# A pooled attention with a gated feed-forward on one core: full-row selections and a re-ordered prologue

## The chip, the core and the metric

The kernel runs on one core of a Trainium2 chip. The metric is device time in microseconds (us) from start to end of one execution. A core has five engines that run their own instruction queues in order and wait for each other through semaphores: TensorE (PE; its weight loads are shown apart as PEld), VectorE (DVE), ScalarE (ACT), GpSimd (POOL) and SyncE (SP). DMAs are issued from the queues of SP, ACT and POOL.

## The reference

Eight batches, eight heads, 576 tokens, head size 64. Keys and values are averaged over groups of eight tokens, so 72 pooled rows remain for each head. The queries attend to them, and the result goes through a feed-forward layer with the activation h / (1 + exp(-h)).

```python
def _attn_ref(q, k, v):
    B, H, S, D = q.shape
    pool = 8
    Sp = S // pool
    scale = 1.0 / np.sqrt(D)
    k_p = k.reshape(B, H, Sp, pool, D).mean(axis=3)
    v_p = v.reshape(B, H, Sp, pool, D).mean(axis=3)
    scores = scale * np.matmul(q, k_p.transpose(0, 1, 3, 2))
    scores = scores - np.max(scores, axis=-1, keepdims=True)
    attn = np.exp(scores)
    attn = attn / (np.sum(attn, axis=-1, keepdims=True) + 1e-09)
    return np.matmul(attn, v_p).astype(np.float32)

def _moe_ref(x, w_in, w_out):
    h = x @ w_in
    g = h * (1.0 / (1.0 + np.exp(-h)))
    return (g @ w_out).astype(np.float32)

def reference(**kwargs):
    ...
    B, H, S, D = attn_out.shape
    x = np.ascontiguousarray(attn_out.transpose(0, 2, 1, 3)).reshape(B * S, H * D)
    return _moe_ref(x=x, **moe_kwargs)
```

The model width is 512, the hidden width 2048, and there are 4608 tokens.

## The kernel before

The tokens are cut into nine tiles of 512 (`NTT`). A tile t is multiplied with `w_in` (function `up`, 16 blocks g of 128 hidden units, Silu on ScalarE into `h_T`), then with `w_out` (`down` for t = 0, `down_quarters` after it, which forms sums of quarters so that seven products do for eight). While tile t goes through these, the attention of batch t + 1 is computed as filler work: a list of (step, function) pairs, where a step is one matmul of the main work. The order of instructions on each engine is therefore the order in which the Python code issues them. The attention of batch 0 stands alone ahead of everything; this is the prologue, written out by hand between the loads and the loop over t (the lines after `act_copy`).

Pooling is done in two ways. For batches 0 to 2 the 576 rows (head, pooled position) of k or v are laid on the 128 partitions in five slots: four full ones and a last one with 64 rows (`SLOTS` = 4, `REST` = 64, `SA` = 3 slots in the first tile, two in the second). `slot_sums` (L274, L278) adds the eight tokens on DVE by halving: for the first three slots 768, 384 and 192 elements a partition, for the last two 512, 256 and 128. Then TensorE picks the rows of each head: `select_k` (L296) multiplies columns of an identity matrix with the sums, and `select_v` (L314) does the same with a shifted identity. A head's 72 rows can lie in two slots (`segments`), so four heads take twelve (k, two halves of a head) or six (v) matmuls. Where a piece lies in the last slot, the matmul has 64 rows, else 128. `a` = 0 or 1 is the half of the heads; only a = 1 reaches the last slot. For batches 3 to 7 pooling is done on 72 partitions and `k_transpose` (L222) transposes the keys on TensorE with 72 rows, into a bf16 PSUM tile.

The attention of a part of the queries is: `q_transpose` (L153, DVE), `scores` (L351, then four exponentials on ACT, L359, one for each s), `denominators` (L369, then a logarithm and an exponential on ACT, L378 and L379, or a reciprocal on DVE, L375), `numerators` (L395, then a multiplication on DVE, L404, into `xT`). In the prologue a part is (head half g, query half f). `copy_k` (L303) and `copy_v` (L321) bring the selected rows from PSUM to SBUF, on ACT or DVE.

PSUM has eight banks: three for the tag `mm`, five for `at`. `warm_up(n)` (L704) issues n matmuls of 128 x 512 on a zero tile whose result nobody reads; they keep TensorE active in the prologue.

In the loop, t = 0 cuts its first `GA` = 11 blocks g in two: the tokens of the first query half (288) for all eleven, then the other 224 for all eleven, then the remaining five blocks with 512. It begins when only the first query half is done. The denominators and numerators of the second half are fillers in it. Before the first Silu, ACT loads another table (L414).

The DMAs of q, of the weights and of part of k and v are issued from GpSimd's queue in program order. An issue on it waits until the DMA eight places before it has landed.

Of the kernel before, what the change touches and what calls it, by code (L numbers as in the profile page):

```python
# [27 lines left out]
FP32 = mybir.dt.float32  # L28
# [8 lines left out]
def kernel(  # L37
# [9 lines left out]
    nc = tc.nc  # L47
# [43 lines left out]
    def ps_tile(shape, dtype, tag, name):  # L91
        return psum.tile(shape, dtype, tag=tag, bufs=banks[tag], name=name)

    shifts = singles.tile([128, SP + 128 + SP], BF16, name="shifts")
    ident = shifts[:, SP : SP + 128]
    ones = singles.tile([SP, 32], BF16, name="ones")
    warm = singles.tile([128, 512], BF16, name="warm")
    w_in_sb = singles.tile([128, KF, d_ff], BF16, name="w_in_sb")  # L100
    w_out_sb = singles.tile([128, KG, d_model], BF16, name="w_out_sb")
    w_sum = singles.tile([128, 5, KQ, CQ], BF16, name="w_sum")
# [14 lines left out]


    kz = [singles.tile([128, 2, 2, SP], BF16, name=f"kz{n}") for n in range(2)]
    gate = singles.tile([128, 1], FP32, name="gate")  # L120

    batches = {}

    def load_q_half(b, f):
        for a in range(2):
            es = slice(f * QF * D, (f + 1) * QF * D)
            nc.gpsimd.dma_start(out=batches[b]["q_bf"][:, a, es], in_=q_r[b][:, a, es])
# [71 lines left out]
    def pool_k(b, stage):  # L199
        st = batches[b]  # L200
        raw = st["k_raw"]
        if stage == 0:
            add_halves(raw)
            return
        st["kp"] = mid.tile([SP, 2, 2, 4, DH], BF16, tag="kp", bufs=1, name="kp")
        for i in range(2):
            add_rest(
                st["kp"][:, i].rearrange("k c s d -> k s c d"), raw[:, 4 * i : 4 * (i + 1)]
            )

    def pool_v(b):
# [4 lines left out]

    def k_transpose(b, parts=(0, 1)):
        st = batches[b]
        kT_ps = ps_tile([128, 2, 2, SP], BF16, "at", "kT_ps")
        for a in parts:  # L220
            for c in range(2):
                nc.tensor.transpose(  # L222
                    kT_ps[:, a, c, :],
                    st["kp"][:, a, c].rearrange("k s d -> k (s d)"),
                    ident[:SP, :SP],
                )
        a0, a1 = parts[0], parts[-1] + 1
        nc.scalar.copy(kz[b % 2][:, a0:a1], kT_ps[:, a0:a1])
# [37 lines left out]
                in_=src[128 * i0 : 128 * i1].rearrange("(i r) e -> r i e", r=128), **how  # L266
            )

    def slot_sums(name, j, halves=False):
        raw = row_tiles[name][j]  # L270
        dst = rows5[name][:, SA:] if j else rows5[name][:, :SA]
        w = RE // 4 if halves else RE // 2
        while w > D:
            nc.vector.tensor_add(  # L274
                out=raw[..., :w], in0=raw[..., :w], in1=raw[..., w : 2 * w]
            )
            w //= 2
        nc.vector.tensor_add(out=dst, in0=raw[..., :D], in1=raw[..., D : 2 * D])  # L278


    def segments(h):
        r = SP * h
        while r < SP * (h + 1):
            i = r // 128
            e = min(SP * (h + 1), 128 * (i + 1))
            yield i, (128 if i < SLOTS else REST), r - 128 * i, r - SP * h, e - r
            r = e

    def select_k(b, a):
        st = batches[b]  # L290
        if a == 0:
            st["kz_ps"] = ps_tile([128, 2, 2, SP], FP32, "at", "kz_ps")
        for c in range(2):
            for s in range(4):
                for i, n, r, sp, m in segments(4 * a + s):
                    nc.tensor.matmul(  # L296
                        st["kz_ps"][32 * s : 32 * (s + 1), a, c, sp : sp + m],
                        lhsT=k5[:n, i, c * DH : (c + 1) * DH],
                        rhs=ident[:n, r : r + m], start=True, stop=True,
                    )  # L300

    def copy_k(b, a, copy=nc.vector.tensor_copy):
# [2 lines left out]
    def select_v(b, a, tag="at"):  # L305
        st = batches[b]
        if a == 0:
            st["v_ps"] = ps_tile([128, H, D], FP32, tag, "v_ps")
            st["vp"] = mid.tile([SP, H, D], BF16, tag="vp", name="vp")
        for h in range(4 * a, 4 * (a + 1)):  # L310
            segs = list(segments(h))
            for j, (i, n, r, sp, m) in enumerate(segs):
                x = SP + r - sp
                nc.tensor.matmul(  # L314
                    st["v_ps"][:SP, h, :], lhsT=shifts[:n, x : x + SP], rhs=v5[:n, i],
                    start=(j == 0), stop=(j == len(segs) - 1),
                )

# [21 lines left out]
            yield g, i0, i1, slice(o, o + n)  # L340
            o += n

    def scores(b, segs):
        st = batches[b]
        w = width(segs)
        sc = [ps_tile([128, 512], FP32, "at", "sc_ps")[:SP, :w] for s in range(4)]
        for g, i0, i1, cs in seg_cols(segs):
            for c in range(2):
                for s in range(4):
                    rows = slice(32 * s, 32 * (s + 1))  # L350
                    nc.tensor.matmul(  # L351
                        sc[s][:, cs],
                        lhsT=kz[b % 2][rows, g, c, :],
                        rhs=st["qT"][rows, g, i0:i1, c, :],
                        start=(c == 0), stop=(c == 1),
                    )
        es = mid.tile([SP, 4, VW], BF16, tag="es", bufs=4, name="es")[:, :, :w]
        for s in range(4):
            nc.scalar.activation(es[:, s, :], sc[s], func=AF.Exp, scale=score_scale)  # L359
        st["es", segs] = es  # L360

# [340 lines left out]
    def warm_up(n):  # L702
        for _ in range(n):
            nc.tensor.matmul(warm_ps, lhsT=warm[:, :128], rhs=warm, start=True, stop=True)  # L704

    load_slots(nc.sync, 0, "k", 0, 2)
    load_slots(nc.scalar, 0, "k", 2, 3)
    load_slots(nc.scalar, 0, "k", 3, 4)
# [1 line left out]
    load_q(0, halves=True)  # L710
    load_q_half(0, 0)
    load_slots(nc.gpsimd, 0, "v", 0, 3)
    load_q_half(0, 1)
    load_slots(nc.gpsimd, 0, "v", 3, 4)
    load_slots(nc.gpsimd, 0, "v", 4, 5)
    attn_tables()
    nc.vector.memset(warm, 0.0)
    nc.vector.memset(ones, float(POOL))
    nc.gpsimd.memset(shifts, 0.0)
    make_identity(nc, ident, nomemset=True)  # L720

# [14 lines left out]
        load_w_in(512 * c, 512 * (c + 1))  # L736

    act_copy = nc.scalar.copy
    warm_up(19)
    slot_sums("k", 0)  # L740
    select_k(0, 0)
    copy_k(0, 0, act_copy)
    warm_up(4)
    q_transpose(0, 0, 0)
    scores(0, part(0, 0))
    slot_sums("k", 1)
    warm_up(3)
    select_k(0, 1)
    copy_k(0, 1, act_copy)
    q_transpose(0, 1, 0)  # L750
    warm_up(2)
    scores(0, part(1, 0))
    denominators(0, part(0, 0))
    slot_sums("v", 0)
    warm_up(2)
    select_v(0, 0, "mm")
    copy_v(0, 0, act_copy)
    denominators(0, part(1, 0))
    q_transpose(0, 0, 1)
    scores(0, part(0, 1))  # L760
    slot_sums("v", 1)
    warm_up(1)
    numerators(0, part(0, 0), ("mm", "at"))
    warm_up(2)
    select_v(0, 1, "mm")
    copy_v(0, 1)
    q_transpose(0, 1, 1)
    warm_up(2)
    numerators(0, part(1, 0), ("mm", "at"))
    scores(0, part(1, 1))  # L770
# [18 lines left out]
    for t in range(NT):  # L789
        a = t + 1  # L790
        f_up, f_down = [], []
        if t == 0:
            GA = 11
            items = [(g, 0, HS) for g in range(GA)]
            items += [(g, HS, NTT - HS) for g in range(GA)]
            items += [(g, 0, NTT) for g in range(GA, KG)]
            f_up += [(1, lambda: denominators(0, part(0, 1), on_dve=True))]
            f_up += [(5, lambda: denominators(0, part(1, 1), on_dve=True))]
            f_up += [(13, lambda: numerators(0, part(0, 1)))]
            f_up += [(17, lambda: numerators(0, part(1, 1)))]  # L800
        else:
            G = lambda *gs: [(g, 0, NTT) for g in gs]
            if t == 1:
                items = (
                    G(12, 13, 14, 15) + [(0, "251")] + G(8) + [(0, "43")] + G(9)
                    + [(0, "7h6")] + G(10) + [(0, "s")] + G(11, 0, 1, 2, 3)
                )
            else:
                items = (
                    G(12, 13) + [(0, "251")] + G(14) + [(0, "43")] + G(15) + [(0, "76")]  # L810
                    + [(1, "2")] + [(0, "hs")] + [(1, "51")] + G(0) + [(1, "43")] + G(1)
                    + [(1, "7h6")] + G(2) + [(1, "s")] + G(3)
                )
            for n in U_X:
                f_up.append((0, lambda n=n: unit_x_sum(t, n)))
            for n in (2, 5):
                f_up.append((36 if t > 1 else 45, lambda n=n: hidden_sum(n, 4, 8)))
            f_up.append((56, lambda: hidden_sum(6, 4, 8)))
            for n, k0 in ((2, 0), (5, 0), (1, 4), (1, 0)):
                f_up.append((64, lambda n=n, k0=k0: hidden_sum(n, k0, k0 + 4)))  # L820
            f_down.append((33, lambda: hidden_sum(7, 0, 8)))
            f_down.append((71, lambda: hidden_sum(6, 0, 4)))
# [99 lines left out]
```

The softmax here doesn't subtract the row's maximum and nothing guards it: scores larger than these inputs give would overflow.

## Time and profile before

| | us |
|---|---|
| median of 3 runs | 286.77 |
| lowest and highest | 286.44 and 287.31 |
| the profiled execution's own time | 286.69 |
| its span, first to last instruction | 284.8 |

The busy times by stage, from a view that cuts the span where the stages change; the columns are the stretch, its length, and each engine's busy time with the number of instructions:

| stretch, us | what | PE busy | DVE | ACT | POOL |
|---|---|---|---|---|---|
| 0 to 22.2 | prologue, first hp blocks | 19.95 | 16.06 | 11.39 | 15.08 |
| 22.2 to 34.7 | t = 0, up | 12.45 | 9.57 | 9.06 | 4.74 |
| 34.7 to 47.5 | t = 0, down | 12.59 | 5.65 | 9.24 | 4.48 |
| 47.5 to 53.8 | end of t = 0 | 6.22 | 6.21 | 1.76 | 2.16 |
| 53.8 to 68 | t = 1, up | 13.97 | 12.61 | 10.40 | 3.56 |
| 68 to 84 | t = 1, down | 16.00 | 13.19 | 10.97 | 3.57 |
| 84 to 284 | t = 2 to 8 | 196.86 | 161.82 | 131.01 | 18.57 |

A busy time of PE counts its dummies, and matmuls overlap, so it is not useful work. Mean granted TensorE clock of the span: 1.000. GpSimd's rows in the prologue are almost all DMA issues. How to read the profile: the chain of waits is followed back from the last instruction to what released it each time, so what stands in it sets the end; the timeline gives start, length and the idle time before a row and who ended it; the DMA issues give the time from issue to landing.

### The profile page before, as it was taken

Reading aid. Unit: us, or ns where it says so; the run is one execution under the profiler, and the core shown is the slowest. Engines: PE = TensorE matmul, PEld = TensorE weight load, DVE = VectorE, ACT = ScalarE, POOL = GpSimd, SP = SyncE. Lnnn points to the kernel's source line nnn. Section 1 sums busy time; section 2 is a strip of 40 time slices with the busy share of each in tenths; the row PEclk is TensorE's granted clock in tenths of the full one; section 3 lists DMA queues with packets and bytes.
Section 4 is the critical chain, followed back from the end, with each engine's and each line's share of the span. In section 5 each row is a group of like instructions: output and inputs, shape, how many; then the busy total and the mean of one; then the engine's idle time right before and its main releaser. Section 6 shows DMA issues by size and latency. Waiting matters only on the chain.

```text
span 284.8 us, 6920 instructions
## 1 busy us (share of the span) xinstructions
PE 278.0 (98%) x2773; PEld 196.0 (69%) x2793; DVE 225.1 (79%) x403; ACT 183.8 (65%) x359; POOL 52.2 (18%) x68
## 2 busy tenths in 40 slices
PE   8989999999999999999999999999999999999995
PEld 3348544465777677767888886677677867787684
DVE  4887854979969796979698969986998686836773
ACT  1577676458656886688568857794779558325700
POOL 8664317402030011101200101054100000000000
PEclk9999999999999999999999999999999999999999
DMA  7999999793849565964895396839970032005004
GB/s 211 277 266 227 219 306 183 214 199 70 153 69 210 124 96 95 145 148 126 140 177 156 72 147 113 176 59 170 150 142 0 2 85 65 2 9 139 1 3 147
DMA packets 35296, 37.70 MB, mean 132 GB/s; under 512 B 9952, under 2 KB 27616, under 8 KB 35264
## 3 DMA queue, kind: packets, MB, share of 16 engines
q0 software_dynamic: 21760, 20.86, 43.0%
q1 hardware_dynamic: 12928, 15.48, 22.2%
q10 hardware_dynamic: 576, 0.92, 0.9%
q8 instruction: 22, 0.36, 0.6%
q14 instruction: 10, 0.08, 0.1%
HBM read 36.70 MB, written 9.44 MB: 162 GB/s over the span
## 4 chain that ended last, share of the span: by engine, by line
PE 94%; DVE 3%; ACT 1%; issue 1%; DVEq 0%
PE hp_ps L547 25%; PE o_psP L655 15%; PE o_psQ L655 15%; PE u_psQ L488 7%; PE u_psP L488 7%; PE o_psR L655 5%; PE sc_ps L351 4%; PE warm_ps L704 4%; PE o_ps L582 3%; PE nu_ps L395 3%; PE u_psR L488 2%; PE den_ps L369 2%; DVE w_sum L633 1%; PE kz_ps L296 1%; DVE xT L404 1%
## 5 line engine op out<-in xcount | busy, mean ns | idle before, releaser
L547 PE MATMUL hp_ps<-xT,w_in_sb 128*128 128x512 bf16 (+3 forms) x397 | 80.8, 338 | 1.4 <-ACT h_T L553 0.4
L655 PEld LDWEIGHTS <-h_sum 128*128 128x128 bf16 x640 | 60.6, 98 | 11.9 <-issue 1.3
L553 ACT ACTIVATE h_T<-hp_ps 128x512 bf16<-128x512 f32 (+2 forms) x95 | 51.4, 546 | 26.3 <-PE hp_ps L547 24.9
L547 PEld LDWEIGHTS <-w_in_sb 128*128 128x128 bf16 x412 | 39.3, 98 | 25.0 <-issue 1.4
L615 DVE TENSOR_TENSOR h_sum<-h_T 128x1024 bf16<-128x1024 bf16 (+1 forms) x72 | 50.8, 743 | 7.0 <-ACT h_T L553 7.0
L359 ACT ACTIVATE es<-sc_ps 72x384 bf16<-72x384 f32 (+1 forms) x100 | 39.0, 470 | 10.0 <-PE sc_ps L351 9.9
L488 PEld LDWEIGHTS <-w_sum 128*128 128x128 bf16 x300 | 29.4, 98 | 7.7
L655 PEld LDWEIGHTS <-h_T 128*128 128x128 bf16 x256 | 24.1, 98 | 4.4 <-issue 0.9
L404 DVE TENSOR_TENSOR xT<-nu_ps,rec 128x384 bf16<-128x384 f32 (+1 forms) x50 | 24.0, 532 | 0.3
L378 ACT ACTIVATE lnd<-den_ps 128x384 f32<-128x384 f32 (+1 forms) x23 | 11.1, 484 | 20.2 <-PE den_ps L369 20.2
L153 DVE STREAM_TRANSPOSE qT<-q_bf 128x576 bf16<-128x576 bf16 x32 | 23.0, 753 | 0.0
L182 POOL DMA_DIRECT2D raw<-in_k_dram x5 | 7.0, 1398 | 79.2 <-DVE h_sum L615 28.8
L496 ACT ACTIVATE h_T<-c_sb 128x512 bf16<-128x512 f32 x30 | 18.1, 625 | 5.0 <-DVE c_sb L520 5.0
L274 DVE TENSOR_TENSOR raw<-raw 128x384 f32<-128x384 f32 (+3 forms) x20 | 12.4, 618 | 7.5 <-DMA raw<-in_v_dram 4.3
L655 PE MATMUL o_psP<-w_out_sb,h_sum 128*128 128x256 bf16 x128 | 17.6, 273 | 0.0
L655 PE MATMUL o_psQ<-w_sum,h_sum 128*128 128x256 bf16 x128 | 16.7, 273 | 0.0
L655 PE MATMUL o_psQ<-w_out_sb,h_sum 128*128 128x256 bf16 x128 | 16.6, 273 | 0.0
L655 PE MATMUL o_psQ<-w_sum,h_T 128*128 128x256 bf16 x128 | 16.5, 273 | 0.0
L655 PE MATMUL o_psP<-w_sum,h_T 128*128 128x256 bf16 x128 | 16.5, 273 | 0.0
L520 DVE TENSOR_TENSOR c_sb<-u_psP,t_sb 128x512 f32<-128x512 f32 x15 | 10.2, 678 | 7.1 <-PE u_psP L488 3.6
L655 PE MATMUL o_psR<-w_sum,h_sum 128*128 128x256 bf16 x128 | 15.7, 273 | 0.0
L655 PE MATMUL o_psP<-w_sum,h_sum 128*128 128x256 bf16 x128 | 15.4, 272 | 0.0
(77 smaller groups left out, 417.1 us busy)
## 6 DMA issues: line engine op xcount, KB each, us to landing
out_dram<-o_sb SPq DMA_DIRECT2D x128, 64.0 KB, 3.0
q_bf<-in_q_dram POOLq DMA_DIRECT2D x6, 576.0 KB, 11.1
raw<-in_k_dram SPq DMA_DIRECT2D x6, 512.0 KB, 5.0
raw<-in_k_dram POOLq DMA_DIRECT2D x5, 576.0 KB, 9.1
raw<-in_v_dram POOLq DMA_DIRECT2D x5, 576.0 KB, 8.6
raw<-in_v_dram SPq DMA_DIRECT2D x5, 512.0 KB, 7.6
w_in_sb<-in_moe_w_in_dram POOLq DMA_DIRECT2D x8, 256.0 KB, 8.4
w_out_sb<-in_moe_w_out_dram POOLq DMA_DIRECT2D x4, 512.0 KB, 13.5
```

The lines of the kernel that those rows point to most:

```text
L153: nc.vector.transpose(out=st["qT"][:, a, f * QF : (f + 1) * QF].rearrange("r i c p -> r (i c p)"), in_=st["q_bf"][:, a, f * n : (f + 1) * n],)
L274: nc.vector.tensor_add(out=raw[..., :w], in0=raw[..., :w], in1=raw[..., w : 2 * w])
L351: nc.tensor.matmul(sc[s][:, cs], lhsT=kz[b % 2][rows, g, c, :], rhs=st["qT"][rows, g, i0:i1, c, :], start=(c == 0), stop=(c == 1),)
L359: nc.scalar.activation(es[:, s, :], sc[s], func=AF.Exp, scale=score_scale)
L404: nc.vector.tensor_mul(out=xT[:, 2 * g0 + c : 2 * (g0 + ng - 1) + c + 1 : 2, cols], in0=nu[c][:, :w].rearrange("r (g n) -> r g n", g=ng), ...
L488: nc.tensor.matmul(ps[bank][:, u, :], lhsT=w[:, kk, 128 * u : 128 * (u + 1)], rhs=x[:, kk, :], start=first and u == 0 and kk == 0, stop=kk ...
L496: nc.scalar.activation(h_T[:, g : g + 2, j * NQ : (j + 1) * NQ], src, func=AF.Silu)
L547: nc.tensor.matmul(hp_ps[:, r0:r1], lhsT=w_in_sb[:, kk, g * 128 : (g + 1) * 128], rhs=xT[:, kk, x0 : x0 + r1 - r0], start=(kk == 0), stop= ...
L553: nc.scalar.activation(h_T[:, g, n0 : n0 + n], hp_ps[:, :n], func=AF.Silu)
L615: nc.vector.tensor_tensor(out=h_sum[n][:, ks, :], in0=quarter(*a, ks), in1=quarter(*b, ks), op=op)
L655: nc.tensor.matmul(ps[b][:, c, :], lhsT=left(n, kt, c), rhs=W_OUT[n][:, kt, :], start=b not in begun, stop=kt == k1 - 1, skip_group_check= ...
L704: nc.tensor.matmul(warm_ps, lhsT=warm[:, :128], rhs=warm, start=True, stop=True)
```

## The change

It has five parts.

- **Rows.** `select_k` and `select_v` always use all 128 rows of a slot (the missing rows of the last slot are zero already). `select_v` also loads 128 columns of the shifted identity instead of 72, so `shifts` becomes wider. `k_transpose` uses all 128 rows of a new tile `kp`, which is zeroed once, and is an ordinary matmul with the identity into an fp32 PSUM tile.
- **Value queue.** In GpSimd's DMA queue the last value slots of batch 0 stand ahead of the second query half.
- **Pool sums.** The sums of batch 0's last two value slots (three additions) are done by GpSimd, behind its six issues for `w_in`, and no longer by DVE.
- **Dummies.** Of the 19 first dummies nine stay; eight fp32 ones of 128 x 128 (`warm_behind`) follow, whose moving operand is the third key slot, so they start when it has landed. Other counts of dummies change too.
- **Order in the prologue.** The second key half (sums, selection, copy) is issued ahead of the fourth exponential of the first part; the value copy goes from ACT to DVE; `q_transpose` and `scores` of the second query half move. `GA` is 12.

```diff
-    shifts = singles.tile([128, SP + 128 + SP], BF16, name="shifts")
+    shifts = singles.tile([128, SP + 256], BF16, name="shifts")
...
+    warm32 = singles.tile([128, 128], FP32, name="warm32")
...
+    kp = singles.tile([128, 2, 2, 4, DH], BF16, name="kp")
...
-        kT_ps = ps_tile([128, 2, 2, SP], BF16, "at", "kT_ps")
+        kT_ps = ps_tile([128, 2, 2, SP], FP32, "at", "kT_ps")
         for a in parts:
             for c in range(2):
-                nc.tensor.transpose(
+                nc.tensor.matmul(
                     kT_ps[:, a, c, :],
-                    st["kp"][:, a, c].rearrange("k s d -> k (s d)"),
-                    ident[:SP, :SP],
+                    lhsT=kp[:, a, c].rearrange("k s d -> k (s d)"),
+                    rhs=ident[:, :SP], start=True, stop=True,
                 )
...
-                        lhsT=k5[:n, i, c * DH : (c + 1) * DH],
-                        rhs=ident[:n, r : r + m], start=True, stop=True,
+                        lhsT=k5[:, i, c * DH : (c + 1) * DH],
+                        rhs=ident[:, r : r + m], start=True, stop=True,
...
-                    st["v_ps"][:SP, h, :], lhsT=shifts[:n, x : x + SP], rhs=v5[:n, i],
+                    st["v_ps"][:, h, :], lhsT=shifts[:, x : x + 128], rhs=v5[:, i],
...
         for s in range(4):
+            if s == 3 and between:
+                between()
             nc.scalar.activation(es[:, s, :], sc[s], func=AF.Exp, scale=score_scale)
...
+    def warm_behind(rhs, n):
+        for _ in range(n):
+            nc.tensor.matmul(
+                warm_ps[:, : rhs.shape[-1]], lhsT=warm32, rhs=rhs, start=True, stop=True
+            )
...
     load_slots(nc.gpsimd, 0, "v", 0, 3)
-    load_q_half(0, 1)
     load_slots(nc.gpsimd, 0, "v", 3, 4)
     load_slots(nc.gpsimd, 0, "v", 4, 5)
+    load_q_half(0, 1)
     attn_tables()
     nc.vector.memset(warm, 0.0)
+    nc.vector.memset(warm32, 0.0)
     nc.vector.memset(ones, float(POOL))
+    nc.vector.memset(kp, 0.0)
...
-    warm_up(19)
+    slot_sums("v", 1, eng=nc.gpsimd)
+    warm_up(9)
+    warm_behind(row_tiles["k"][0][:, SA - 1, RE - 128 :], 8)
     slot_sums("k", 0)
     select_k(0, 0)
     copy_k(0, 0, act_copy)
     warm_up(4)
     q_transpose(0, 0, 0)
-    scores(0, part(0, 0))
-    slot_sums("k", 1)
-    warm_up(3)
-    select_k(0, 1)
-    copy_k(0, 1, act_copy)
+
+    def rest_k():
+        slot_sums("k", 1)
+        warm_up(3)
+        select_k(0, 1)
+        copy_k(0, 1, act_copy)
+
+    scores(0, part(0, 0), rest_k)
     q_transpose(0, 1, 0)
     warm_up(2)
     scores(0, part(1, 0))
     denominators(0, part(0, 0))
     slot_sums("v", 0)
+    warm_up(3)
+    select_v(0, 0, "mm")
+    copy_v(0, 0)
+    denominators(0, part(1, 0))
     warm_up(2)
-    select_v(0, 0, "mm")
-    copy_v(0, 0, act_copy)
-    denominators(0, part(1, 0))
     q_transpose(0, 0, 1)
-    scores(0, part(0, 1))
-    slot_sums("v", 1)
-    warm_up(1)
     numerators(0, part(0, 0), ("mm", "at"))
     warm_up(2)
+    scores(0, part(0, 1))
+    warm_up(2)
     select_v(0, 1, "mm")
+    q_transpose(0, 1, 1)
     copy_v(0, 1)
-    q_transpose(0, 1, 1)
     warm_up(2)
     numerators(0, part(1, 0), ("mm", "at"))
     scores(0, part(1, 1))
...
-            GA = 11
+            GA = 12
```

More of the change, by code (lines that the diff above doesn't have):

```diff
@@ L119 @@
     kz = [singles.tile([128, 2, 2, SP], BF16, name=f"kz{n}") for n in range(2)]
-    gate = singles.tile([128, 1], FP32, name="gate")
+    kp = singles.tile([128, 2, 2, 4, DH], BF16, name="kp")
     batches = {}
@@ L204, in pool_k @@
             return
-        st["kp"] = mid.tile([SP, 2, 2, 4, DH], BF16, tag="kp", bufs=1, name="kp")
         for i in range(2):
             add_rest(
-                st["kp"][:, i].rearrange("k c s d -> k s c d"), raw[:, 4 * i : 4 * (i + 1)]
+                kp[:SP, i].rearrange("k c s d -> k s c d"), raw[:, 4 * i : 4 * (i + 1)]
             )
@@ L267, in load_slots, with slot_sums @@
             )
-    def slot_sums(name, j, halves=False):
+    def slot_sums(name, j, halves=False, eng=nc.vector):
         raw = row_tiles[name][j]
@@ L273, in slot_sums @@
         while w > D:
-            nc.vector.tensor_add(
+            eng.tensor_add(
                 out=raw[..., :w], in0=raw[..., :w], in1=raw[..., w : 2 * w]
@@ L277, in slot_sums @@
             w //= 2
-        nc.vector.tensor_add(out=dst, in0=raw[..., :D], in1=raw[..., D : 2 * D])
+        eng.tensor_add(out=dst, in0=raw[..., :D], in1=raw[..., D : 2 * D])
     def segments(h):
@@ L285, in segments @@
             e = min(SP * (h + 1), 128 * (i + 1))
-            yield i, (128 if i < SLOTS else REST), r - 128 * i, r - SP * h, e - r
+            yield i, r - 128 * i, r - SP * h, e - r
             r = e
@@ L294, in select_k @@
             for s in range(4):
-                for i, n, r, sp, m in segments(4 * a + s):
+                for i, r, sp, m in segments(4 * a + s):
                     nc.tensor.matmul(
                         st["kz_ps"][32 * s : 32 * (s + 1), a, c, sp : sp + m],
-                        lhsT=k5[:n, i, c * DH : (c + 1) * DH],
-                        rhs=ident[:n, r : r + m], start=True, stop=True,
+                        lhsT=k5[:, i, c * DH : (c + 1) * DH],
+                        rhs=ident[:, r : r + m], start=True, stop=True,
                     )
@@ L311, in select_v @@
             segs = list(segments(h))
-            for j, (i, n, r, sp, m) in enumerate(segs):
+            for j, (i, r, sp, m) in enumerate(segs):
                 x = SP + r - sp
                 nc.tensor.matmul(
-                    st["v_ps"][:SP, h, :], lhsT=shifts[:n, x : x + SP], rhs=v5[:n, i],
+                    st["v_ps"][:, h, :], lhsT=shifts[:, x : x + 128], rhs=v5[:, i],
                     start=(j == 0), stop=(j == len(segs) - 1),
@@ L341, in seg_cols, with scores @@
             o += n
-    def scores(b, segs):
+    def scores(b, segs, between=None):
         st = batches[b]
```

## The prediction, made before the changed kernel ran

> **What bounds the kernel now.** I read the page's first section, then the chain of waits over the first 30 us and over the whole run, then the timeline of TensorE, ScalarE and GpSimd in the stages that the change touches, then the DMA issues for landing times.
>
> ```profile
> PE 278.0 (98%) x2773; PEld 196.0 (69%) x2793; DVE 225.1 (79%) x403; ACT 183.8 (65%) x359; POOL 52.2 (18%) x68
> ```
>
> TensorE is busy for 98% of the span, and its list of waits over the whole run adds up to 2.6 us, all but 0.4 before 22 us. From there to the end (DVE is in the chain only between 47 and 54 us, released by TensorE) a TensorE cycle saved is time saved. Before 22 us this is false: many of its matmuls are dummies on `warm_ps`. There the chain of waits shows who sets the end:
>
> ```profile
> 1.20 6.84 PE warm_ps L704 x19
> ...
> 15.80 0.42 DVE vp L321
> 16.23 0.69 DVE qT L153
> 16.96 0.48 PE sc_ps L351 x8
> 17.44 1.29 ACT es L359 x4
> 18.75 1.28 ACT L414
> 20.03 0.01 issue
> 20.04 0.42 ACT h_T L553
> 20.46 0.04 issue
> 20.50 0.40 PE hp_ps L547 x2
> ```
>
> The reader should see that the prologue ends when the last exponentials (`es`) and the table load let the first Silu free a PSUM bank; TensorE resumes at 20.50. Behind that chain stands the value half: DVE sums the last value slots from 13.48 to 14.95, then `select_v`, `copy_v`, a query transpose, scores.
>
> The second place is the price of 64-row matmuls among 128-row ones, in TensorE's timeline:
>
> ```profile
> 28.23 0.28 PE L296 MATMUL kz_ps<-shifts,k 128*32 128x72 bf16 x12
> 28.43 0.94 PE L547 MATMUL hp_ps<-xT,w_in_sb 128*128 128x224 bf16 x8
> 29.30 0.64 PE L296 MATMUL kz_ps<-shifts,k 128*32 128x72 bf16 x12
> 29.88 1.49 PE L547 MATMUL hp_ps<-xT,w_in_sb 128*128 128x224 bf16 x9
> ...
> 45.31 0.37 PE L314 MATMUL v_ps<-v,shifts 128*72 128x64 bf16 x6
> 45.52 0.81 PE L582 MATMUL o_ps<-w_out_sb,h_T 128*128 128x512 bf16 x3
> 46.19 0.48 PE L314 MATMUL v_ps<-v,shifts 128*72 128x64 bf16 x6
> 46.60 0.60 PE L582 MATMUL o_ps<-w_out_sb,h_T 128*128 128x512 bf16 x2
> ```
>
> Start to start, twelve key selections with 128 rows take 0.20 us (28.23 to 28.43); the twelve that hold two 64-row pieces take 0.58 (29.30 to 29.88). Six value selections take 0.21, and with one 64-row piece 0.41.
>
> **What the Trainium skill says.** (1) TensorEngine Tiling (Array Packing), Key Properties: changing the tiling mode drains TensorE. The trace agrees: (0.58-0.20)/2 = 0.19 us per 64-row piece, 0.20 for the value one. (2) GPSIMD Engine Reference, 3.1: a two-input fp32 add of 2048 elements takes 4497 ns there against 2293 on DVE, so 2.2 ns an element; no run here shows a GpSimd add. (3) The same page, 2.1: a first call to a freshly loaded kernel costs about 6 us (5.95) that no row shows; not seen here either. (4) FP8 and Floating Point Precision, TensorE Precision Notes: true fp32 is four passes through the array; no fp32 matmul is in this trace.
>
> **The change, part by part.**
>
> *Full rows in the selections.* The 64-row pieces after the prologue are: two in batch 1's keys (29.30), one in its values (46.19), two in batch 2's keys (58.67 to 59.57 for all 24, where the stretch also holds a matmul whose record is missing), one in its values (73.99 to 74.61 = 0.62 for twelve against 2 x 0.21). All stand in dense TensorE work. Saved: 0.38 + 0.20 + 0.38 + 0.20 = 1.16 us. Value weights grow from 72 to 128 columns: the transposes on L222 already load 128 columns, and four of them fit between hp matmuls that start 0.35 apart, where one matmul of 512 takes 0.22, so about 33 ns each, against 35 for a value selection. No charge.
>
> *Key transposes (L222) with 128 rows and fp32 PSUM.* 72 rows already ran without a drain (33 ns each), so nothing is gained; ScalarE's copy of 128x288 took 417 ns from bf16, and an fp32 activation of 128x288 takes 411. Zero, both ways; 20 matmuls at worst 0.05 us each bound it at 1 us, which I do not take.
>
> *GA 11 to 12.* One 512 item (4 x 0.216 = 0.86) becomes 4 x 0.122 + 4 x 0.096 = 0.87. ScalarE pays 411 + 358 instead of 594 ns, hidden, since TensorE needs 0.49 and 0.38 for such items. +0.01.
>
> *Value queue.* The two q pieces of the second half (landing at about 10.9 and 11.8) now come behind the last value slots (issued 4.31 and 4.84, landing 8.6 and 8.5 later, so 12.9 and 13.3). The first value block lands at 2.46 + 7.7 = 10.2 as before. The q pieces took 11.8 - 10.2 = 1.6 us of the queue, so the slots land at about 11.3 and 11.8, q at 12.5 and 13.4.
>
> *Last value slots on GpSimd.* Its queue: six w_in issues, the fifth and sixth now waiting for the value pieces instead of q. The sixth started at 12.07 and ended at 12.78; the slots are in by 11.8, so it still ends at about 12.8. The adds cover 512 + 256 + 128 = 896 elements a partition: 896 x 2.2 = 1.97 us, plus three fixed parts of 0.1 (the smallest GpSimd rows are 93 to 96 ns) and two waits of its own: P = 2.5 us, an estimate from that page; bounds 2.0 and 3.5. The end is 15.3, against 14.95 on DVE before. Queued behind are batch 1's key loads (before 13.45, now 15.3), q and the last w_in. Ahead of them five w_in of 256 KB still fill the DMA engines until about 21 us, and their own waits were later anyway, so landings stay.
>
> *From there to the Silu.* Before, value selection at 15.22 to the copy's end at 16.22 was 1.00, now 0.88 (0.12 to 0.2 of drain gone); the query transpose no longer stands between copy and scores. Sum: 15.3 + 0.06 + 0.88 + 0.06 + nu 0.40 = 16.7 for the last scores, against 16.96. Gain 0.26. In terms of P: shift = 12.8 + P + 1.4 - 16.96 = P - 2.76.
>
> *Dummies and first key half.* Nine bf16 dummies at 0.427 (the spacing of the first weight loads of `warm`, before the clock rises) end at 1.20 + 3.84 = 5.04; the gating ACT DMA landed by 5.28 at the latest, when DVE began. Eight fp32 128x128 in four passes stream what a 512-column dummy streams: three cold (the clock rose at about 6.3) and five warm give 3 x 0.43 + 5 x 0.22 = 2.4, so 7.4. Key selection then starts at 7.4 instead of 7.97 (keys summed at 7.23). Bounds: 7.3, and 10.5 if every pass also exposes a weight load of 98 ns.
>
> *Key half 1 before the fourth exponential, value copy from ACT to DVE.* With selection at S, es of (0,0) starts at S + 1.64, three of them, copy 0.28, the fourth; es of (1,0) at S + 3.5, four (1.30), two ln/rec pairs (2 x 0.86) and es of (0,1) can start at S + 6.5, ending 1.3 later. The last exponentials start at 16.7 + 0.47 = 17.17, so S may be as late as 9.3. DVE has room: copy_v 0.42 at about 12.7, q transpose 0.77 at 13.1, xT 0.8, q transpose to 15.5, before the copy at 15.8. (0,1) scores start at about 14.2. No gain here beyond the 0.26, no loss up to S = 9.3.
>
> *Does the gain survive?* Last w_in lands at 18.30 + 11.2 = 29.5; its first item starts at about 31.5, so it allows 2.0 us. The last w_out lands at 28.45 + 14.6 = 43.05, needed at 45.52. A gain of 1.4 fits.
>
> **Sum**: -1.16 - 0.26 + 0.01 = -1.41 on the profiled execution's 286.69 us (span 284.8 and 1.9 around it) = 285.3. The median is 286.77, 0.08 more; also 285.3 or 285.4.
>
> **Rivals.**
> - *GpSimd is the bound (slower).* Place: the three adds before `select_v(0,1)`. Net = P - 2.76 - 1.15 = P - 3.91. It decides from P = 3.9 (nothing gained) and 4.8 (slower by 0.3%). With the 5.95 us first-call cost P = 8.45: +4.5, 291.2. For: GpSimd does no arithmetic add in the trace, and all the slack of 1.3 us on ScalarE before the last exponentials hangs on it. Against: no loading instruction is added, and of what that page's section 1 names as a contender for the shared SBUF interface, DVE instructions with two SBUF inputs, none runs on DVE in those microseconds.
> - *The fp32 dummies are long.* At 1.0 us each, S = 13.05, 3.75 past the limit: 289.0. For: unseen in the trace. Against: needs over 0.53 each.
> - *Only half arrives.* If DVE or ScalarE take over where TensorE is earlier (DVE is 6.2 of 6.3 us busy from 47.5 to 53.8), perhaps the two drains before that stretch (0.58) are lost and the prologue gives nothing: 286.1. Against: DVE there idles 2.74 us just before, waiting for TensorE.
>
> **Chances.** Forecast 0.56; half 0.20 (mostly within the bound); GpSimd long 0.16; dummies long 0.08. About 0.3% (0.86 us) is what a measurement can tell from no change. Faster 0.60, within 0.18, slower 0.22. The likeliest's own range is 284.5 to 286.0 (P from 2.0 to 3.2); for 8 in 10 I go from 284.3 to 288.0, which leaves out the load case and the longest dummies.
>
> **What would show it.** Right: L296 groups of twelve all followed by hp 0.2 us later; no 64-row form; GpSimd adds ending near 15.3; hp resuming near 20.2. Wrong: GpSimd adds past 16.7, the key selection after 9.3, or a DMA wait ahead of the last w_in item.

## The result, and the profile after

The changed kernel takes 286.92 us (median of 6 runs, 286.41 to 288.37), the kernel before 286.93 (6 runs on the same chip, 286.44 to 287.33). The ratio is 1.0007, with a 95% interval of 0.9982 to 1.0031: no change that can be told. The profiled execution took 286.91 us, with a span of 285.0, against 286.69 and 284.8 before. A gain of 1.41 was forecast.

Most of what the prediction said would show in the trace is there. First TensorE's timeline of the changed kernel (start, length, row), where the prologue's dummies and batch 1's key selections stand:

```profile
1.20 3.68 PE L706 MATMUL warm_ps<-warm 128*128 128x512 bf16 x9 [1.20 <-DVE warm L725]
4.98 2.02 PE L710 MATMUL warm_ps<-raw,warm 128*128 128x128 f32 x16
7.28 0.28 PE L296 MATMUL kz_ps<-shifts,k 128*32 128x72 bf16 x12 [0.28 <-DVE k L278]
...
28.20 0.28 PE L296 MATMUL kz_ps<-shifts,k 128*32 128x72 bf16 x12
28.41 0.94 PE L549 MATMUL hp_ps<-xT,w_in_sb 128*128 128x224 bf16 x8
29.28 0.29 PE L296 MATMUL kz_ps<-shifts,k 128*32 128x72 bf16 x12
29.51 2.26 PE L549 MATMUL hp_ps<-xT,w_in_sb 128*128 128x224 bf16 x18
```

Both groups of twelve key selections now give way after 0.21 and 0.23 us; before, the second held TensorE for 0.58. The gated dummies end at 7.0; the first key selection waits 0.28 us more, for VectorE's key sums, and starts at 7.28.

The chain of waits of the changed kernel through the prologue:

```profile
3.23 8.05 DMA raw<-in_v_dram
11.27 0.29 issue
11.56 1.42 POOL w_in_sb L737 x2
12.99 0.02 issue
13.01 1.29 POOL raw L274
...
14.37 0.73 POOL raw L274
...
15.19 0.46 POOL v L278
...
17.31 1.29 ACT es L361 x4
...
19.91 0.42 ACT h_T L555
```

GpSimd's sums run from 13.01 to 15.65, and the first Silu (`h_T`) starts at 19.91, where it started at 20.04. The whole start now hangs on the landing of the value slots and GpSimd's queue: the chain runs through GpSimd, where before it ran through TensorE's queue, dummies included, up to 15.7. The fifth `w_in` issue, the twelfth on that queue, begins 0.29 us after the fourth, a value slot, has landed at 11.27.

The difference is lost 120 us later. Here is VectorE's timeline at the end of tile 3, first before, then after:

```profile
140.35 0.69 DVE L686 TENSOR_TENSOR o_sb<-o_psP,t_sb 128x512 f32<-128x512 f32 x1 [1.11 <-PE o_psP L655]
140.98 1.02 DVE L404 TENSOR_TENSOR xT<-nu_ps,rec 128x384 bf16<-128x384 f32 x2
142.05 1.22 DVE L188 TENSOR_TENSOR raw<-raw 72x1024 f32<-72x1024 f32 x1
143.31 0.76 DVE L193 TENSOR_TENSOR kp<-raw 72x256 bf16<-72x256 f32 x2
143.99 0.68 DVE L690 TENSOR_TENSOR o_sb<-o_psQ,t_sb 128x512 f32<-128x512 f32 x1
144.59 1.75 DVE L455 TENSOR_TENSOR x_sum<-xT 128x512 bf16<-128x512 bf16 x5
```

```profile
139.40 0.69 DVE L688 TENSOR_TENSOR o_sb<-o_psP,t_sb 128x512 f32<-128x512 f32 x1 [1.11 <-PE o_psP L657]
140.02 1.02 DVE L406 TENSOR_TENSOR xT<-nu_ps,rec 128x384 bf16<-128x384 f32 x2
142.33 1.22 DVE L189 TENSOR_TENSOR raw<-raw 72x1024 f32<-72x1024 f32 x1 [1.29 <-DMA raw<-in_k_dram]
143.59 0.76 DVE L194 TENSOR_TENSOR kp<-raw 72x256 bf16<-72x256 f32 x2
144.27 0.68 DVE L692 TENSOR_TENSOR o_sb<-o_psQ,t_sb 128x512 f32<-128x512 f32 x1
144.87 1.42 DVE L457 TENSOR_TENSOR x_sum<-xT 128x512 bf16<-128x512 bf16 x4
```

At 140 us the changed kernel is 0.95 us ahead (139.40 against 140.35). Then VectorE, in order, comes to the first addition of `pool_k` for batch 5 and waits 1.29 us for the keys. Before, it arrived at 142.00 and began at 142.05: no wait, and no slack either, for the second half of these keys was issued at 132.91 and took 9.1 us to land. Behind the addition stand `kp`, `o_sb` and the five `x_sum` that the next tile's products need, so TensorE stops as well (the view of after ends before the fifth begins). The list of TensorE's waits from 84 to 284 us, empty before, has one line:

```profile
PE u_psR L490 <- DVE x_sum L457: 1.0, 1, 1.0
```

From there on the changed kernel is 0.2 to 0.3 us behind the kernel before.

### The profile page after: what moved, and what is told of

Same layout as the page of the kernel before. It is cut to its first block, busy times and chain, and to the rows that moved or that the text cites. A ratio compares the mean times of both kernels' runs of the same rounds, so it can differ in the third digit from the quotient of the medians.

```text
span 285.0 us, 6970 instructions
## 1 busy us (share of the span) xinstructions
PE 277.7 (97%) x2807; PEld 195.5 (69%) x2807; DVE 224.5 (79%) x403; ACT 184.0 (65%) x359; POOL 54.6 (19%) x71
## 4 chain that ended last, share of the span: by engine, by line
PE 88%; DMA 3%; DVE 3%; POOL 2%; ACT 1%; issue 1%; SPq 1%; DVEq 0%; POOLq 0%
PE hp_ps L549 25%; PE o_psP L657 15%; PE o_psQ L657 15%; PE u_psQ L490 7%; PE u_psP L490 7%; PE o_psR L657 5%; PE sc_ps L351 4%; PE o_ps L584 3%; DMA raw<-in_v_dram 3%; PE nu_ps L397 2%; PE u_psR L490 2%; PE den_ps L371 2%; DVE w_sum L635 1%; DVE xT L406 1%; POOL raw L274 1%
## 5 line engine op out<-in xcount | busy, mean ns | idle before, releaser
L549 PE MATMUL hp_ps<-xT,w_in_sb 128*128 128x512 bf16 (+3 forms) x416 | 82.6, 338 | 0.5 <-ACT h_T L555 0.4
L183 POOL DMA_DIRECT2D raw<-in_v_dram x5 | 6.9, 1390 | 50.9 <-DVE kp L194 23.6
L274 DVE TENSOR_TENSOR raw<-raw 128x384 f32<-128x384 f32 (+3 forms) x18 | 11.2, 623 | 6.7 <-DMA raw<-in_v_dram 3.9
L657 PE MATMUL o_psR<-w_sum,h_sum 128*128 128x256 bf16 x128 | 15.7, 273 | 0.0
```

The lines of the kernel that those rows point to most:

```text
L183: nc.gpsimd.dma_start(out=batches[b][f"{name}_raw"], in_=source(b, name)[:, :, PH:], accum_op=ALU.add,)
L274: eng.tensor_add(out=raw[..., :w], in0=raw[..., :w], in1=raw[..., w : 2 * w])
L549: nc.tensor.matmul(hp_ps[:, r0:r1], lhsT=w_in_sb[:, kk, g * 128 : (g + 1) * 128], rhs=xT[:, kk, x0 : x0 + r1 - r0], start=(kk == 0), stop= ...
L657: nc.tensor.matmul(ps[b][:, c, :], lhsT=left(n, kt, c), rhs=W_OUT[n][:, kt, :], start=b not in begun, stop=kt == k1 - 1, skip_group_check= ...
```

## The experiments

Theory M: the gain is real, and is given back where VectorE waits for the keys of batch 5. The rival R: it is lost in the change's own parts, or to DMA bandwidth as such, so another late transfer takes the wait over. Ratios are to the kernel before, run beside it on the same chip.

**1. The key load from another queue.** Each key load has two halves: the first from SyncE's queue behind 16 stores, the second an accumulation that GpSimd issues when the first has landed.

```diff
-        load_rows(nc.sync, raw, source(b, name)[:, :, :PH])
+        load_rows(nc.scalar if name == "k" else nc.sync, raw, source(b, name)[:, :, :PH])
```

> The changed kernel, but the first half of each key load (batches 3 to 7) is issued from ScalarE's queue at the start of a tile instead of from SyncE's, where it stood behind 16 stores. Theory M (the 1.1 to 1.3 us were gained and are given back where VectorE waits for the keys of batch 5 to land, 142.31): the first half is issued some 7 us earlier (near 116.5 for batch 5 instead of 123.97), the keys land by 139, the waits of L189 for raw and of u_psR for x_sum near 145 go, and the time is 1.1 us below before, 285.8. Rival R (the time is lost in the change's own parts or through DMA bandwidth, so another late transfer takes the wait over): the time stays at 286.9 within 0.3, with a new wait of about 1 us somewhere behind 140.

Measured: 318.99 us, ratio 1.1138 (1.1104 to 1.1171). The same edit on the kernel before:

> The kernel before with the same move of the first half of each key load to ScalarE's queue. M: before never waited for keys by more than 0.1 us, so nothing is gained: 286.8, within 0.3. If instead it gains about as much as the changed kernel does by this edit (1.1 us), the key load was a bound of both kernels and not the place where the gain of the change goes.

Measured: 319.55 us, 1.1135 (1.1095 to 1.1174). Both theories missed. The list of waits of the first of the two names the cause:

```profile
ACT h_T L555 <- DMA out_dram<-o_sb: 27.8, 4, 7.3
```

ScalarE's next Silu, behind the load in its queue, waits for stores to land: the issue of the load has taken its place behind the 16 stores' landings with it, and holds ScalarE for up to 7.3 us in each of four tiles. In the chain of waits of that run, a store issued at 84.02 lands at 92.27, the load's second piece is issued at 92.29, and the Silu starts at 92.62. The run says nothing of M.

**2. The pooling of the keys later.**

```diff
+                for stage in range(2):
+                    f_up.append((6, lambda stage=stage: pool_k(a, stage)))
                 f_up.append((22, lambda: k_transpose(a)))
...
-                for stage in range(2):
-                    f_down.append((100, lambda stage=stage: pool_k(a + 1, stage)))
-                f_up.append((0, lambda: load_one(a + 1, "k")))
+                f_up.append((7 if t > 1 else 0, lambda: load_one(a + 1, "k")))
...
-                f_up.append((2, lambda: load_rest(a + 1, "k")))
+                f_up.append((9 if t > 1 else 2, lambda: load_rest(a + 1, "k")))
```

> The changed kernel, with the pooling of the keys (L189, L194; batches 4 to 7, for batch 3 too where it is used from tile 2 on) moved from step 100 of a tile's second half to step 6 of the next tile's first half, behind x_sum, and the next key load behind it. The keys may then land about 3 us later before anything waits, and x_sum no longer stands behind them. M: the wait of u_psR for x_sum goes, 285.8, as in the first run, by another way; the following key loads start 3 us later, and if one of them is late again the gain is only part, 286.2. R: 286.9.

Measured: 289.12 us, 1.0085 (1.0070 to 1.0100). TensorE's list of waits after 20 us begins:

```profile
PE u_psQ L490 <- DVE rr_sb L510: 3.2, 5, 0.6
PE hp_ps L549 <- ACT h_T L555: 0.4, 1, 0.4
```

The wait for `x_sum` is gone, but the pooling now stands ahead of `rr_sb`, which costs 0.6 us in each of five tiles. The profiled 288.98 less 3.2 is 285.8, M's number, but that is a subtraction and not a measurement.

**3. The key load ahead of half of the stores.** The load stays on SyncE's queue and is issued right behind the pooling that frees its buffer. No other engine's order changes.

```diff
-                f_up.append((0, lambda: load_one(a + 1, "k")))
+                if t == 1:
+                    f_up.append((0, lambda: load_one(a + 1, "k")))
+                if a + 2 < B:
+                    f_down.append((101, lambda: load_one(a + 2, "k")))
```

> The changed kernel with the first half of the key load one step behind the pooling that frees its buffer (step 101 of the tile before), still on SyncE's queue, so ahead of the last 8 stores of that tile instead of behind them; nothing moves on TensorE, VectorE and ScalarE. Theory M (the gain is given back where VectorE waits for the keys of batch 5): issued near 118 instead of 123.97, keys landed near 137, no wait of L189 for raw and none of u_psR for x_sum, 285.6 to 285.8, and a narrower spread of the times. Rival R (the changed prologue loses what the rows bring, wherever the keys land): 286.9.

Measured: 285.18 us (284.93 to 285.70), 0.9927 (0.9910 to 0.9944). SyncE's timeline of the changed kernel, and then of this one:

```profile
111.69 11.75 SPq L569 DMA_DIRECT2D out_dram<-o_sb  x14
123.97 1.70 SPq L174 DMA_DIRECT2D raw<-in_k_dram  x2
131.66 1.19 SPq L174 DMA_DIRECT2D raw<-in_v_dram  x2
```

```profile
111.94 6.56 SPq L569 DMA_DIRECT2D out_dram<-o_sb  x6
118.61 1.28 SPq L174 DMA_DIRECT2D raw<-in_k_dram  x2
121.36 5.22 SPq L569 DMA_DIRECT2D out_dram<-o_sb  x8
131.76 1.19 SPq L174 DMA_DIRECT2D raw<-in_v_dram  x2
```

The load is issued 5.4 us earlier, and VectorE finds the keys there:

```profile
139.49 0.69 DVE L688 TENSOR_TENSOR o_sb<-o_psP,t_sb 128x512 f32<-128x512 f32 x1 [1.11 <-PE o_psP L657]
140.12 1.02 DVE L406 TENSOR_TENSOR xT<-nu_ps,rec 128x384 bf16<-128x384 f32 x2
141.06 1.21 DVE L189 TENSOR_TENSOR raw<-raw 72x1024 f32<-72x1024 f32 x1
```

The addition starts 1.27 us earlier than in the changed kernel, without a wait, and TensorE has no wait at all from 84 to 284 us. M holds and R falls: a single load, issued earlier, gives 1.7 us (286.92 to 285.18). The two traced executions lie 1.21 us apart (286.91 and 285.70), which is the wait. The median fell by more, below M's 285.6 to 285.8; what else the load brings in executions without a trace is not shown.

The same edit on the kernel before:

> The kernel before with the same earlier issue of the key load. M: before stood at zero slack (keys landed at 142.03, VectorE ready at 142.00), so a part of its executions may wait a little: 286.4 to 286.8, a gain of at most 0.4, and a narrower spread than the 285.9 to 288.0 of before. R says nothing of it. If it gains 1 us or more, the key load bounds the kernel before as well, by more than its profile shows.

Measured: 286.13 us (285.89 to 286.60), 0.9957 (0.9938 to 0.9977). The gain of 0.91 is more than M's 0.4: so the kernel before, too, seems to lose something to this load in most executions, though the profiled one shows no such wait. A further trace of it:

> The kernel before once more, for a second trace. Its executions here lie between 286.1 and 289.4. M: where an execution is above about 286.7, VectorE waits for the keys of batch 5 (or 6) in it, as in the changed kernel, and where it is below, not. Rival (the earlier key load helped the kernel before through something else): no such wait in an execution of 287 or more.

Measured: 286.39 us (one run). Its prologue was quicker (first Silu at 19.36, not 20.04), and VectorE waited for the next batch's keys:

```profile
170.90 1.22 DVE L188 TENSOR_TENSOR raw<-raw 72x1024 f32<-72x1024 f32 x1 [0.39 <-DMA raw<-in_k_dram]
```

Its lead over the first trace of before falls there from 0.74 to 0.36 us, so an earlier start is clipped in the kernel before as well. M had put the border at 286.7; here a wait shows at 286.39. An execution of 287 or more was not caught in a trace.

**4. The parts of the change alone.** Full rows with the old prologue (the first two hunks of the diff without `warm32`, the row and `k_transpose` edits, and the zeroing of `kp`):

> The kernel before with full rows in the selections and key transposes alone; prologue, dummies and value queue as before. M: about 0.7 to 1.1 us ahead of before between 80 and 140 us, then the same wait for the keys of batch 5, which land where before had them (142.0 to 142.3): 286.7 to 287.0. Rival (the changed prologue's order of issues makes the key loads late): the keys land about 1 us before 142.03, no wait, 285.7.

Measured: 286.46 us (285.05 to 287.19, 22 runs), 0.9981 (0.9969 to 0.9992). Its profiled execution took 285.40, with this row:

```profile
140.74 1.22 DVE L188 TENSOR_TENSOR raw<-raw 72x1024 f32<-72x1024 f32 x1 [0.40 <-DMA raw<-in_k_dram]
```

The median lies between M's and the rival's number; in the traced execution the keys happened to land at 140.7, and most of the gain came through. With the earlier load:

> Full rows alone with the earlier key load. M: the 1.16 us of the drains arrive in every execution: 285.5 (before with the same load less 1.0 to 1.2), with a spread below that of full rows alone (285.05 to 287.19). R: no wait was what spread the times of full rows alone: again about 286.4.

Measured: 284.91 us (284.80 to 285.22), 0.9922 (0.9905 to 0.9940). Against before with the same load that is -1.22, and the spread falls from 2.1 to 0.4 us: most of the spread of full rows alone (22 runs, against 5 here) was the keys' landing, as M has it.

The changed prologue alone (all the rest of the diff):

> The changed prologue (value queue, Pool sums, dummies, order, GA 12) without full rows. M: 0.13 to 0.26 earlier at 20 us; its w_in and batch 1 to 2 loads come up to 2.3 us later on GpSimd's queue, and so may later keys: 286.6 to 287.2, a wait for keys at 142 of at most 0.5. R: the prologue costs about 0.5 to 1.2 us somewhere, as the changed kernel at 286.9 against full rows alone at 286.46 hints: 287.3 to 288.0.

Measured: 287.45 us (286.67 to 288.47, 22 runs), 1.0015 (1.0003 to 1.0027). Here R was nearer: the new prologue costs. Its traced execution, one of the slowest (288.30), has the key wait too, 1.34 us from 142.27 on, more than the 0.5 that M allowed, although at 140 us it was behind before, not ahead. So in this execution the keys also landed later. How much of the 0.4 us is this wait is open: the prologue alone with the earlier load was not run.

The eight traces side by side: the first Silu (start of the first `h_T`), VectorE's `o_sb` row at the end of tile 3 shown above, the time between the two, and the wait for batch 5's keys:

| kernel | first Silu | `o_sb` | between | wait for keys | profiled us |
|---|---|---|---|---|---|
| before | 20.04 | 140.35 | 120.31 | 0 | 286.69 |
| before, again | 19.36 | 139.68 | 120.32 | 0 | 286.39 |
| before, early load | 19.76 | 140.08 | 120.32 | 0 | 286.26 |
| prologue alone | 20.17 | 140.63 | 120.46 | 1.34 | 288.30 |
| full rows | 19.39 | 138.69 | 119.30 | 0.40 | 285.40 |
| full rows, early load | 19.19 | 138.49 | 119.30 | 0 | 284.80 |
| changed | 19.91 | 139.40 | 119.49 | 1.29 | 286.91 |
| changed, early load | 20.18 | 139.49 | 119.31 | 0 | 285.70 |

Full rows bring 1.02 us between the first Silu and 140 us, in each of their traces to within 0.2. The loss can be read off as cleanly: from this `o_sb` row to the same row a tile later takes 29.18 us in the second trace of before and in the three traces with the early load, 29.25 in the first trace of before, and 30.48, 30.53 and 29.60 in the changed kernel, the prologue alone and full rows, which waited 1.29, 1.34 and 0.40.

The starts scatter. Three of the runs above add traces of the same prologues: the key load from ScalarE, 19.38 (changed) and 19.57 (before), and the later pooling, 19.51 (changed). So the old prologue ends at 19.36 to 20.04 (four traces, mean 19.68), with full rows at 19.19 and 19.39, and the new one at 19.38 to 20.18 (five, mean 19.83). In the old one the first Silu comes 12.06 or 12.07 us behind the first key selection, which starts anywhere from 7.30 to 7.97 (the chains of waits put it down to the dummies ahead of it or to the keys' landing), and with full rows 12.03 and 11.89; in the new one it comes 6.9 to 7.0 us behind the start of GpSimd's sums, which start at 12.48 to 13.29.

**5. What holds the new prologue.** All three runs have the earlier key load. GpSimd's sums put back on VectorE, behind its first value sums:

```diff
-    slot_sums("v", 1, eng=nc.gpsimd)
...
     slot_sums("v", 0)
+    slot_sums("v", 1)
     warm_up(3)
```

> The changed kernel with the earlier key load, and with the sums of the last value slots back on VectorE, directly behind those of the first slots. Theory P (in the changed prologue the value slots' landing, GpSimd's two w_in issues and the 2.6 us of its sums are the chain that sets the first Silu): the sums end near 13.5 instead of 15.6 to 15.9, the last exponentials start near 16.4 instead of 17.3 to 17.6, and the time is 0.6 to 0.9 us below 285.18, near 284.4. Rival (something else in the new order, such as its dummies or the value copy on VectorE, holds the prologue): 285.0 to 285.4.

Measured: 285.35 us (285.21 to 285.68), 0.9938 (0.9924 to 0.9951): nothing gained, the rival's number. The chain of waits of this kernel:

```profile
13.13 0.29 DVE v L278
13.43 0.34 DVE vp L321
13.77 0.04 issue
13.81 0.43 PE nu_ps L397 x8
14.24 0.54 PE warm_ps L706 x2
14.78 0.37 PE sc_ps L351 x8
15.15 0.54 PE warm_ps L706 x2
15.68 0.19 PE v_ps L314 x6
```

The sums end at 13.42, as expected, but the selection of the last values comes behind the first numerators, scores and four dummies in TensorE's queue, and starts at 15.68. Sums on GpSimd in front of the last two `w_in` issues:

```diff
-    for c in range(3):
+    for c in range(2):
         load_w_in(512 * c, 512 * (c + 1))
+    slot_sums("v", 1, eng=nc.gpsimd)
+    load_w_in(1024, 1536)
...
-    slot_sums("v", 1, eng=nc.gpsimd)
```

> The changed kernel with the earlier key load; GpSimd's sums stay, but stand ahead of the fifth and sixth w_in issue instead of behind them. P: the sums start near 11.6 instead of 13.0 to 13.3 and end near 14.2, 1.4 us earlier; the last exponentials start near 16.2; those two w_in land up to 2.6 us later, which the first hp blocks of the third quarter may feel. 284.3 if they do not, 285.2 if they do. Rival: 285.0 to 285.4 with the Silu start unmoved.

Measured: 285.02 us (284.63 to 285.23), 0.9921 (0.9908 to 0.9935). The first Silu comes at 19.07, between 0.3 and 1.1 us earlier than in the five traces with the sums behind the issues, so in that order GpSimd's queue was the bound. But TensorE now reaches the last `w_out` before it lands. Issued at 28.90, it landed at 44.2, about when it did in the changed kernel with the early load (28.56 and 44.3), where TensorE came later:

```profile
PE o_ps L584 <- DMA w_out_sb<-in_moe_w_out_dram: 0.5, 1, 0.5
```

Against the changed kernel with the early load (285.18) the two are not told apart. The last run takes the better half of the change and another order in the old prologue: no values ahead of the last scores.

```diff
     scores(0, part(0, 1))
+    q_transpose(0, 1, 1)
     slot_sums("v", 1)
...
     copy_v(0, 1)
-    q_transpose(0, 1, 1)
+    scores(0, part(1, 1))
     warm_up(2)
     numerators(0, part(1, 0), ("mm", "at"))
-    scores(0, part(1, 1))
```

> Full rows and the earlier key load (284.91), with the old prologue in another order: the last query transpose ahead of the last value sums on VectorE, and the last scores ahead of the numerators, so that the last exponentials need no values. Theory Q (the last exponentials and the table load behind them set the first Silu): they start near 15.3 instead of 16.58, the first Silu near 18.2 unless its hp waits for xT, and TensorE has up to 1.2 us more; the last w_out, which lands at 43.10 and is needed near 44.2, lets through about 1.1: 284.0 to 284.3, perhaps with a short wait for w_out. Rival (xT or a dummy count holds the first hp blocks): 284.7 to 285.1.

Measured: 284.43 us (284.21 to 284.66), 0.9912 (0.9890 to 0.9935), the fastest of all, between Q's number and the rival's. ScalarE's timeline:

```profile
14.29 2.68 ACT L358 ACTIVATE es<-sc_ps 72x288 bf16<-72x288 f32 x8
17.00 1.28 ACT L413 ACT_TABLE_LOAD   x1
18.29 0.41 ACT L552 ACTIVATE h_T<-hp_ps 128x288 bf16<-128x288 f32 x1
18.90 0.90 ACT L552 ACTIVATE h_T<-hp_ps 128x288 bf16<-128x288 f32 x2 [0.20 <-PE hp_ps L546]
```

The exponentials run through, and the first Silu comes 0.9 us earlier than with full rows and early load alone. Half of that arrives (284.91 to 284.43); the second Silu already waits for its hp. No wait for `w_out` shows.

## Why the prediction was wrong

- **"Does the gain survive?" is the step that failed.** It asked only whether the last `w_in` and the last `w_out` land in time, and both did. It didn't ask the same of the loads that each tile makes for the batch after next. The trace of before had the answer in two rows of VectorE: its `xT` ended at 142.00 and the addition behind it, which needs the keys, began at 142.05, as they landed. In the changed kernel the second half of the keys was issued 1.9 us earlier, at 131.03, but took 11.3 us instead of 9.1, so it landed at 142.3 while VectorE was free at 141.04. Freed of this wait by one earlier load, the change is worth 0.95 us of the 1.41 forecast (286.13 to 285.18); without it, nothing.
- **Full rows: right.** Forecast -1.16 for the drains after the prologue, measured -1.02 between the first Silu and 140 us. The Trainium skill's statement (TensorEngine Tiling, Key Properties) that changing the tiling mode drains TensorE agrees: without the 64-row pieces, the second twelve selections hold it for 0.23 us instead of 0.58.
- **The prologue: GpSimd's sums were sized rightly, the gain was not there.** P was put at 2.5 and is 2.6, and the first Silu, forecast at 20.04 - 0.26 = 19.78, came at 19.83 in the mean of five traces. But 20.04 was one execution, and the latest of four; their mean is 19.68. Against it the new prologue is 0.15 late, well inside the scatter of both (0.7 and 0.8 us). The times agree: of the 0.95 us, 1.02 are the rows', which leaves 0.07 lost. Moving the sums off VectorE could not bring much by itself: before, they were ready at 14.95, but the chain of waits ran through TensorE's queue, whose selection of the last values began at 15.22. Nor is the new prologue better than the old one with full rows: with the early load 285.18 against 284.91, ranges overlapping.
- **Dummies: the forecast held for another reason.** Selection at 7.28 (forecast 7.4). But the gated dummies took 2.02 us and not 2.4; they were done at 7.0, and what the selection waited for were the key sums, which ended at 7.23.
- **GA, key transposes: no cost seen.** With the rows in and the early load, the time between first Silu and 140 us is 119.31 with GA 12 and 119.30 with GA 11 (119.49 in the trace of the changed kernel itself). Near 147.5 us four transposes stand between hp matmuls that start 0.24 us apart, before and after.
- **The rivals.** "Only half arrives" had the right shape and the wrong place: it put the takeover at VectorE near 50 us, where 0.7 us of the lead went through unharmed. "GpSimd is the bound" decided from P = 3.9 and didn't come about, yet its chain is the one that sets the start.
- **What stays open.** Why the keys land at 142.3 in the changed kernel and at 140.7 with full rows alone: their second half is issued at 131.03 and 131.21, and takes 11.3 and 9.5 us. In both, the first half of the values is issued within a microsecond of it and runs beside it (9.6 and 5.6 us). With the early load the second half of the keys stands 4.9 us ahead of the values and took 7.4 us, but other transfers moved too, so the cause is not isolated. That the slower executions of the kernel before wait longer for keys is inferred from what the earlier load gives, not seen in a trace.

## What to carry to other kernels

Before a saving on the busiest engine is booked, find every row further on that starts right behind its neighbour and also needs a DMA: its slack is the time between that landing and the moment the engine is free, and in this kernel it was zero. A transfer that is issued behind others in a queue moves only as far as the queue does, so moving one load up may be worth more than the instructions saved (here 1.7 us against 1.2). And take the start of a prologue from several executions before a gain of a few tenths is measured against it: here one and the same prologue scattered by 0.7 us.

## What the runs showed of the hardware

- GpSimd's additions took 1.29, 0.73 and 0.46 us for 512, 256 and 128 elements a partition, so 2.2 ns for each further element and some 0.17 us fixed. That agrees with the price in the Trainium skill (GPSIMD Engine Reference, 3.1), which gave 2.2 for one long addition. The first-call cost of 5.95 us that its section 2.1 states for a freshly loaded kernel doesn't show in these additions: the first started 0.02 us behind the issue before it.
- Eight fp32 matmuls of 128x128 appear as 16 rows of TensorE and take 2.02 us, 0.25 each on average. The skill's four passes (FP8 and Floating Point Precision, TensorE Precision Notes) can't be counted in the trace; two rows a matmul can.
- An issue put on ScalarE's queue held its arithmetic for up to 7.3 us until stores issued from SyncE had landed. These waits add up to 27.8 us in the trace, and the run took 32 us longer, at a granted clock of 0.961.
